# Transposing q and k of the later head pairs as float32r words by way of a DRAM copy, with a rearranged start

## The chip, the cores and the metric

One core of a Trainium2 chip runs the whole program. The metric is the device time of one execution in microseconds (us). The median of three runs of the kernel before is 1066.27 us (1065.2 to 1066.96).

## The reference, cut to what matters

Attention over 4 batches, 8 heads, 576 tokens and head size 64, with a memory term mixed in by a gate, then two feed-forward stages on the 2304 rows that result. All of it is float32.

```python
scores = scale * (q @ k.T)                 # causal, then softmax -> a
local  = a @ v
q_p    = phi(q)                            # elu(q) + 1
mem    = (q_p @ M_prev) / (q_p @ z_prev)
x      = g * mem + (1 - g) * local         # g = sigmoid(beta), per head
h      = relu(x @ w_in);  y = (s * h * h + b) @ w_out
out    = (sigmoid(y @ w_gate) * (y @ w_val)) @ w_out2
```

## The kernel before, in words

The work on attention is cut into 16 jobs, one for each batch and pair of heads. Two heads of 64 make one tile of 128 columns, and the 576 tokens make five blocks (four of 128 and a last of 64, in which the two heads share the partitions). Jobs 0 to 3 (batch 0) are called DIRECT and have their own code (`prep_direct`, L989, `scores_direct`, `products_direct`); jobs 4 to 15 go through `plan_prep` (L541), `plan_scores` and `plan_products`. For each job, `load_raw` (L389) brings q, k and v from DRAM with 64-float rows. `transposed` (L444) then turns the five blocks of q and the five of k on TensorE, with the float32 identity `ident` as the moving operand and the block as the stationary one (L451), into PSUM. ScalarE writes the rounded high half of the result (`q_hi`, `k_hi`), VectorE the remainder (`q_lo`, `k_lo`), both as float32r, and every later product is three float32r matmuls on high and low halves.

The feed-forward products follow: `h_mm` (L320, matmuls at L326), in 128 chunks of 12 matmuls, which are also the filler that TensorE does between attention steps from about 87 us on; y (L1519); then the gate and value products m (L1787) and the output o (L1884). The rectified h goes through a ring of two tiles `r` (L335), each for two chunks, and is stored to DRAM by SyncE (`h_store`, L338).

The order is not written by hand. Each step is put into a `Plan` with its engine, an estimated duration and an urgency; `order()` (L70) plays it through and, whenever an engine is free, takes the most urgent step that is ready by these estimates. The urgencies come from the numbers in `TUNE` (L24). The resulting order of each engine is fixed in the program: a step whose data comes late holds all that stands behind it on its engine, SyncE's queue of DMA issues included. The slots (`slots`, L468) bound how far loads run ahead: two tiles each for raw q and raw k.

Before the plan starts, `load_consts` (L218) issues three small broadcasts from ScalarE's queue (beta, s, b), and computes the gates; `load_consts2` (L377) spreads them with twelve small VectorE copies. The first q (job 0) is loaded from ScalarE's queue behind these three, all other loads from SyncE's.

Of the kernel before, what the change touches and what calls it, by code (L numbers as in the profile page):

```python
# [13 lines left out]
ALU = mybir.AluOpType  # L14
# [142 lines left out]
def attention_moe_kernel(  # L157
# [36 lines left out]
    def dram(name, shape):  # L194
        return nc.dram_tensor(name, shape, F32, kind="Internal").ap()

    r_d = dram("relu_scratch", [DFF, NT])
# [8 lines left out]
    ident = const.tile([P, P], F32, name="ident")  # L206
    nc.gpsimd.memset(ident, 0.0)
    nc.gpsimd.affine_select(
        out=ident, in_=ident, compare_op=ALU.not_equal, fill=1.0, base=0,
        pattern=[[-1, P]], channel_multiplier=1,  # L210
    )
    gt = const.tile([P, H], F32, name="gt")
# [5 lines left out]
    def load_consts():  # L218

        nc.scalar.dma_start(gt, beta.partition_broadcast(P))  # L220
        nc.scalar.dma_start(sb_s, s_in.partition_broadcast(P))
        nc.scalar.dma_start(sb_b, b_in.partition_broadcast(P))
        nc.scalar.activation(gt, gt, AF.Exp, scale=-1.0)
        nc.vector.tensor_scalar(out=gt, in0=gt, scalar1=1.0, scalar2=None, op0=ALU.add)
# [120 lines left out]
    rawqs = [at.tile([P, NQ, P], F32, name=f"rawq{i}", bufs=1) for i in range(2)]  # L345
    rawks = [at.tile([P, NQ, P], F32, name=f"rawk{i}", bufs=1) for i in range(2)]
    rawv = at.tile([P, NQ, P], F32, name="rawv", bufs=1)

    def zero_raw():


        for t in rawks:
            nc.gpsimd.memset(t[LAST:, NQ - 1], 0.0)
        for t in rawqs:
            for e in range(2):
                nc.gpsimd.memset(t[e * LAST : (e + 1) * LAST, NQ - 1, (1 - e) * D : (2 - e) * D], 0.0)
        nc.gpsimd.memset(rawv[: P - LAST, NQ - 1], 0.0)

# [18 lines left out]
    def load_consts2():  # L377
        for e in range(2):
            c = slice(e * NQ, e * NQ + NT4)
            nc.vector.tensor_copy(iom[:, :, c], iomg[:, e::2].unsqueeze(2).broadcast_to([P, NP, NT4]))  # L380
            r = slice(e * LAST, (e + 1) * LAST)
            nc.vector.tensor_copy(iom[r, :, NT4], iomg[r, e::2])
            for dst, src in ((iomu, iomg), (gtu, gt)):
                nc.vector.tensor_copy(
                    dst[:, :, e : 2 * NT4 : 2], src[:, e::2].unsqueeze(2).broadcast_to([P, NP, NT4])
                )
                nc.vector.tensor_copy(dst[r, :, NC - 1], src[r, e::2])

    def load_raw(j, src, dst, ta):  # L389
        b, p, t0, t1 = jobs[j]  # L390
        eng = nc.scalar if src is q and j == 0 else nc.sync
        te = min(t1, NQ - 1)
        d4 = dst if len(dst.shape) == 4 else dst.rearrange("p t (h d) -> p t h d", h=2)
        for e in range(2):
            eng.dma_start(
                d4[:, ta:te, e],
                src[b, 2 * p + e, ta * P : te * P].rearrange("(t p) d -> p t d", p=P),
            )
        if t1 == NQ and src is q:
# [84 lines left out]
    def flip(n):  # L484
        return 112 * n + 30
# [1541 lines left out]
```

## Time and profile before

| | |
|---|---|
| median of 3 runs | 1066.27 us |
| the profiled execution's own time | 1065.1 us |
| its span | 1063.0 us |
| TensorE busy | 1037.5 us, 98% |
| TensorE idle in the span | 25.5 us |
| VectorE, ScalarE, GpSimd busy | 696.1, 564.4, 315.0 us |

The span runs from the first to the last instruction that the profiler recorded. The profiled execution took 2.1 us more than its span and 1.2 us less than the median. Busy times of TensorE are unions of pipelined matmuls, so a group's busy time has a tail of the last matmul in it; the chain of waits tells better how long a group holds the engine.

### The profile page before, as it was taken

What the parts mean: (1) busy time and instruction counts of PE and PEld (TensorE: products, weight loads), DVE (VectorE), ACT (ScalarE), POOL (GpSimd) and SP (SyncE); (2) the same over time, 40 slices, a digit from 0 to 9 for tenths busy, and PEclk for the clock granted to TensorE, in tenths of its full rate; (3) what the DMA queues carried; (4) which work ended last, traced back from release to release, by engine and by line L of the source; (5) the groups of instructions that cost most, each with busy time, mean ns of one, the idle gap of its engine ahead of it and who ended that gap; (6) DMA issues with size and microseconds to landing.
All of it is one profiled execution on the core that took longest, in us unless ns stands there. A gap on an engine that the chain in (4) does not pass through costs nothing.

```text
span 1063.0 us, 18848 instructions
## 1 busy us (share of the span) xinstructions
PE 1037.5 (98%) x6696; PEld 979.9 (92%) x6696; DVE 696.1 (65%) x1424; ACT 564.4 (53%) x1221; POOL 315.0 (30%) x361
## 2 busy tenths in 40 slices
PE   4998999999999999999999999999999999999998
PEld 3887999999999999999999999998899998899986
DVE  4887888866667638669888775778525576155531
ACT  3877778876777748557777673335212243112230
POOL 2244665554343503310400002446102342033200
PEclk9999999999999999999999999999999999999999
DMA  6533444333321129659689977992368830677400
GB/s 154 135 103 91 122 138 123 82 105 87 89 80 57 51 93 320 210 195 331 235 289 364 389 260 261 329 343 79 114 216 256 251 111 30 199 253 256 154 24 36
DMA packets 159693, 186.45 MB, mean 175 GB/s; under 512 B 70256, under 2 KB 135280, under 8 KB 159600
## 3 DMA queue, kind: packets, MB, share of 16 engines
q1 hardware_dynamic: 157952, 184.95, 53.9%
q8 instruction: 53, 0.87, 0.3%
q10 hardware_dynamic: 1648, 0.30, 0.2%
q14 instruction: 40, 0.33, 0.1%
HBM read 138.03 MB, written 47.19 MB: 174 GB/s over the span
## 4 chain that ended last, share of the span: by engine, by line
PE 95%; ACT 2%; DVE 2%; issue 1%; DMA 1%; POOL 0%; ACTq 0%; DVEq 0%; POOLq 0%
PE m L1787 24%; PE h L326 19%; PE y L1519 18%; PE o L1884 14%; PE sc L704 3%; PE o L1251 2%; PE acc L888 2%; PE acc L889 2%; PE pt_B L835 1%; PE sc L730 1%; PE sc L1118 1%; PE kt L451 1%; PE qt L451 1%; PE acc L892 1%; PE pt_D L835 1%
## 5 line engine op out<-in xcount | busy, mean ns | idle before, releaser
L1787 PE MATMUL m<-yt,ws 128*128 128x384 f32 x1512 | 262.8, 334 | 0.0
L1787 PEld LDWEIGHTS m<-yt,ws 128*128 128x128 f32 x1512 | 262.2, 188 | 0.3
L326 PE MATMUL h<-x,w_in 128*128 128x256 f32 (+1 forms) x1536 | 224.9, 300 | 0.0
L326 PEld LDWEIGHTS h<-x,w_in 128*128 128x128 f32 x1536 | 209.2, 190 | 2.9 <-issue 1.8
L1799 DVE TENSOR_TENSOR set<-m,set 128x384 f32<-128x384 f32 x252 | 135.6, 555 | 99.7 <-PE m L1787 91.7
L1884 PE MATMUL o<-w_out,ps 128*128 128x512 f32 x648 | 152.1, 396 | 0.6 <-DVE ps L1874 0.6
L1519 PE MATMUL y<-gh,w_out 128*128 128x384 f32 (+1 forms) x768 | 150.7, 338 | 0.7 <-ACT r L336 0.5
L1884 PEld LDWEIGHTS o<-w_out,ps 128*128 128x128 f32 x648 | 121.7, 188 | 29.9 <-DVE ps L1874 1.0
L1519 PEld LDWEIGHTS y<-gh,w_out 128*128 128x128 f32 x768 | 135.4, 188 | 1.4 <-ACT r L336 0.8
L1809 POOL TENSOR_TENSOR p<-set,set 128x384 f32<-128x384 f32 x72 | 75.6, 1056 | 187.8 <-DVE set L1799 186.8
L278 POOL TENSOR_TENSOR w_out<-raw_w_out,w_out 128x512 fp32r<-128x512 f32 x28 | 37.8, 1350 | 214.3 <-DVE set L1799 127.8
L336 ACT ACTIVATE r<-h 128x320 f32<-128x320 f32 (+1 forms) x128 | 52.3, 410 | 71.5 <-PE h L326 59.1
L684 DVE CUSTOM_DVE_ANT_0 P<-sc,mask 128x256 f32<-128x256 f32 (+4 forms) x144 | 68.4, 514 | 24.1 <-PE sc L704 19.7
L1519 PE MATMUL y<-gl,w_out 128*128 128x384 f32 x384 | 82.9, 337 | 0.0
L1795 ACT COPY set<-m 128x384 f32<-128x384 f32 x36 | 17.3, 481 | 111.5 <-PE m L1787 111.5
L762 POOL TENSOR_SCALAR P<-P,rs 128x384 f32<-128x384 f32 (+4 forms) x108 | 64.7, 621 | 30.4 <-DVE rs L758 18.8
L1504 DVE TENSOR_TENSOR gl<-rr,gh 128x384 fp32r<-128x384 f32 x96 | 57.7, 609 | 22.5 <-PE y L1519 12.5
L1874 DVE TENSOR_TENSOR ps<-p,ps 128x512 fp32r<-128x512 f32 x54 | 46.1, 883 | 35.8 <-ACT ps L1861 35.5
L1519 PEld LDWEIGHTS y<-gl,w_out 128*128 128x128 f32 x384 | 68.6, 188 | 0.0
L746 ACT ACTIVATE P<-P,nm 128x384 f32<-128x384 f32 (+4 forms) x108 | 62.6, 581 | 10.1 <-DVE nm L684 9.8
L1803 ACT ACTIVATE set<-set 128x384 f32<-128x384 f32 x72 | 37.6, 524 | 57.1 <-DVE set L1799 57.1
L1861 ACT CAST ps<-p 128x512 fp32r<-128x512 f32 x54 | 31.9, 620 | 65.8 <-PE o L1884 51.8
(185 smaller groups left out, 1507.2 us busy)
## 6 DMA issues: line engine op xcount, KB each, us to landing
ws<-weight_scratch SPq DMA_DIRECT2D x108, 512.0 KB, 4.6
rr<-relu_scratch SPq DMA_DIRECT2D x96, 192.0 KB, 5.4
weight_scratch<-wp SPq DMA_DIRECT2D x36, 512.0 KB, 6.5
raw_w_out<-in_moe_w_out_dram SPq DMA_DIRECT2D x28, 512.0 KB, 5.6
relu_scratch<-r SPq DMA_DIRECT2D x32, 320.0 KB, 2.7
ws<-weight_scratch SPq DMA_DIRECT2D x36, 256.0 KB, 3.0
raw_w_in<-in_moe_w_in_dram SPq DMA_DIRECT2D x16, 512.0 KB, 4.2
relu_scratch<-r SPq DMA_DIRECT2D x32, 256.0 KB, 2.4
```

The costliest lines, as they stand in the source:

```text
L326: nc.tensor.matmul(t[:, :n], wt[:, wi, c], x[:, xi, c], start=(m == 0), stop=(m == 3 * NK - 1))
L336: nc.scalar.activation(rts[b, c0, f - f % 2][:, f % 2, :n], t[:, :n], AF.Relu)
L684: nc.vector.tensor_tensor_reduce(out=pr, in0=ps, in1=mk, scale=1.0, scalar=3e38, op0=ALU.add, op1=ALU.min, accum_out=nm,)
L746: nc.scalar.activation(pr, pr, AF.Exp, bias=T.pop(("nm", j, e, t)), scale=-1.0, accum_out=T["sums", j][:, col : col + 1],)
L762: nc.gpsimd.tensor_scalar(out=pr, in0=pr, scalar1=T["rs", j, part][:, n : n + 1], scalar2=1.0, op0=ALU.mult, op1=ALU.mult,)
L1504: nc.vector.tensor_tensor(out=gl, in0=r_sb.pop(step)[:, :n], in1=gs[step][0][:, :n].bitcast(F32), op=ALU.subtract,)
L1519: nc.tensor.matmul(accs[wi][d][:, : y.shape[1]], w_out_sb[f][:, x, d], y, start=(f == 0 and x == 0 and y is gh), stop=(f == NF - 1 and y i ...
L1787: nc.tensor.matmul(acc, wt[:, a, k : k + P], yt[:, y, c], start=(m == 0), stop=(m == 3 * K2 - 1),)
L1799: nc.vector.tensor_tensor(out=t[:, o], in0=Z["m", z, x], in1=t[:, i], op=ALU.add)
L1809: engine[TIMES[o]].tensor_tensor(out=p[:, f + HF * OF[o][0], OF[o][1]], in0=Z["set", z][:, o], in1=Z["set", zg][:, o], op=ALU.mult,)
L1874: nc.vector.tensor_tensor(out=part(t, 1, i), in0=src(i), in1=part(t, 0, i).bitcast(F32), op=ALU.subtract,)
L1884: nc.tensor.matmul(Z["zo", z], Z["ps", z, i][:, a, k * P : (k + 1) * P], w_out2_sb[f][:, x].rearrange("p c f -> p (c f)"), start=(i == k = ...
```

## The change

1. **Later jobs (4 to 15).** q and k of a job are first copied from DRAM to DRAM (`copy`, one DMA of 294,912 bytes for each of q and k), then loaded from that scratch into tiles of type float32r. `transposed` sees the type and transposes with a float32r identity (`identr`) into a float32r view of PSUM. phi reads the same words as float32.
2. **One comparison.** For job 4 the first four blocks of k are also transposed in float32 (`again`), and VectorE compares 32 columns of both (`compare`, four small instructions); where they differ, 1e30 is added to b.
3. **DIRECT jobs (0 to 3).** q and k are loaded with four tokens to a partition, in runs of 256 floats instead of 64; the transposes write every fourth column of PSUM (`mixed`), which puts the tokens in order again. In job 0 the transposed q is taken in two parts (four blocks and one). The high half of q comes ahead of the rectified copy on ScalarE.
4. **Constants.** The three broadcasts go to SyncE's queue and into the plan; the twelve copies go to GpSimd (`spread`). `mem_norm`, `norm`, `phi_s` and `rsums` now wait for the gates.
5. **The plan.** all 39 numbers in `TUNE` have new values and three are added, so the order on all engines is played out anew. The estimates of the q and k transposes of the later jobs go from 112 to 58 ns per block.

```diff
@@ transposed
-            nc.tensor.transpose(t[:, c : c + P], src[:, i], ident)
+            o = t[:, i : NT4 * P : NT4] if mixed and i < NT4 else t[:, c : c + P]
+            if src.dtype == F32R:
+                nc.tensor.transpose(o.bitcast(F32R), src[:, i], identr)
+            else:
+                nc.tensor.transpose(o, src[:, i], ident)
@@ load_raw
+        tokens = "(p t) d -> p t d" if j in DIRECT and src is not v else "(t p) d -> p t d"
...
+        if from_q or from_k:
+            dst = raw_of("q" if from_q else "k", j)
+            if j not in DIRECT:
+                dst, src = dst.bitcast(F32), qs_d if from_q else ks_d
...
+    def copy(j, src):
+        b, p = jobs[j][:2]
+        h = slice(2 * p, 2 * p + 2)
+        nc.sync.dma_start((qs_d if src is q else ks_d)[b, h], src[b, h])
@@ plan_load
+            bounce = not direct and src is not v
+            if bounce:
+                add(
+                    "SP", 450, lambda src=src: copy(j, src), u + du + AT["cp"],
+                    reads=[("ld", j - 2)], writes=[(key + "d", j)], late=1900, size=3e5,
+                )
@@ plan_prep
-        add("PE", flip(nt), qt, u + AT["q"], reads=[("rawq", j)],
+        add("PE", 58 * nt + 30, qt, u + AT["q"], reads=[("rawq", j)],
...
+        def again():
+            T["ka", j] = transposed(raw_of("k", j).bitcast(F32), 0, NT4, f"ka{j}")
...
+        if j == NP:
+            add("PE", flip(NT4), again, u + AT["k"], reads=[("rawk", j)], new=[("s", ("ka", j))], late=250)
@@ load_consts
-        nc.scalar.dma_start(gt, beta.partition_broadcast(P))
-        nc.scalar.dma_start(sb_s, s_in.partition_broadcast(P))
-        nc.scalar.dma_start(sb_b, b_in.partition_broadcast(P))
+        nc.sync.dma_start(gt, beta.partition_broadcast(P))
+        nc.sync.dma_start(sb_s, s_in.partition_broadcast(P))
+        nc.sync.dma_start(sb_b, b_in.partition_broadcast(P))
@@ prep_direct
+        parts = [(t0, NT4), (NT4, t1)] if j == 0 else [(t0, t1)]
...
+        add("ACT", act(n) + more, q_hi, u + AT["q"], reads=qts, writes=[("QT", j)])
+        add("ACT", act(n) + more, relu, u + AT["q"], reads=qts, writes=[("phi", j)])
@@ the plan
+    add("SP", 1500, load_consts, AT["lc"], writes=[("gates", 0)], late=1900)
+    add("ACT", 210, gate_exp, AT["gc"], writes=[("gates", 0)])
+    add("DVE", 1000, gates, AT["gc"], writes=[("gates", 0)])
+    for x in range(4):
+        add("POOL", 600, lambda x=x: spread(x), AT["gc"], writes=[("gates", 0)])
...
-    load_consts()
-    load_consts2()
@@ TUNE (some of the 42 values)
-    "mem": -121814.8, ... "ft": -153978.3, "m": 1612.8, ... "relu": -411.9, "wo": 957.8, ... "gv": 152484.7,
+    "mem": -261434.9, ... "ft": -264268.8, "m": -86465.6, ... "relu": -158690.1, "wo": -4845.2, ... "gv": 193.7,
```

## Rows read from the trace of the kernel before

**Rows 1.** The page: busy time by engine, and TensorE in 40 slices

```profile
PE 1037.5 (98%) x6696; PEld 979.9 (92%) x6696; DVE 696.1 (65%) x1424; ACT 564.4 (53%) x1221; POOL 315.0 (30%) x361
...
PE   4998999999999999999999999999999999999998
...
GB/s 154 135 103 91 122 138 123 82 105 87 89 80 57 51 93 320 210 195 331 235 289 364 389 260 261 329 343 79 114 216 256 251 111 30 199 253 256 154 24 36
```

**Rows 2.** Busy time by stage (stretch, length, engines, clock, DMA share, GB/s)

```profile
0.00:9.20 9.20, 0.00 (x0) 0.03 (x1) 2.32 (x17) 1.49 (x2) 4.16 (x22) 1.00 0.51 101
9.20:26.00 16.80, 11.28 (x65) 8.55 (x65) 9.07 (x26) 7.49 (x13) 1.31 (x1) 1.00 0.70 179
26.00:106.00 80.00, 74.75 (x683) 65.90 (x684) 66.26 (x185) 61.21 (x130) 30.55 (x38) 0.98 0.44 111
106.00:372.00 266.00, 265.42 (x2120) 250.40 (x2119) 194.51 (x486) 198.43 (x501) 133.14 (x168) 1.00 0.33 93
```

**Rows 3.** What TensorE waited for, whole span (us, times, longest)

```profile
PE qt L451 <- DMA mem<-in_z_prev_dram: 9.2, 1, 9.2
PE ret L1063 <- DVE phi L1019: 3.0, 1, 3.0
PE pt_B L835 <- POOL P L762: 2.1, 1, 2.1
PE kt L451 <- DVE KT L1040: 1.5, 1, 1.5
```

**Rows 4.** q and k transposes: the tile views, and the chain around 321 us

```profile
L451 PE MATMUL qt<-ident,rawq x80: 270/273/477, 9.2 to 321.6; 128*128 128x128 f32 x80
...
L451 PE MATMUL kt<-ident,rawk x80: 270/273/476, 15.8 to 329.9; 128*128 128x128 f32 x80
...
321.35 0.55 PE qt L451 x5
...
329.62 0.55 PE kt L451 x5
```

**Rows 5.** Timeline of TensorE at 308 us: float32r matmuls with 128 columns

```profile
308.35 0.22 PE L888 MATMUL acc<-PT_A,VHL 128*128 128x128 f32 x1
308.41 0.22 PE L889 MATMUL acc<-PT_A,VHL 128*64 128x128 f32 x1
308.47 0.33 PE L892 MATMUL acc<-FS,mst 128*128 128x256 f32 x1
```

**Rows 6.** Timeline of the first 20 us, the queues and the first steps

```profile
0.74 0.45 ACTq L220 DMA_DIRECT2D gt<-in_beta_dram  x1
...
1.23 0.52 ACTq L221 DMA_DIRECT2D sb_s<-in_moe_s_dram  x1
...
1.78 0.52 ACTq L222 DMA_DIRECT2D sb_b<-in_moe_b_dram  x1
...
2.33 0.46 ACTq L395 DMA_DIRECT2D rawq<-in_q_dram  x1
...
4.06 0.61 SPq L406 DMA_DIRECT2D rawk<-in_k_dram  x1
...
5.72 0.38 ACTq L395 DMA_DIRECT2D rawq<-in_q_dram  x1
...
5.98 0.35 SPq L433 DMA_DIRECT2D mem<-in_M_prev_dram  x1
...
6.49 1.17 ACTq L401 DMA_DIRECT2D rawq<-in_q_dram  x2
...
9.21 1.30 PE L451 MATMUL qt<-ident,rawq 128*128 128x128 f32 x5 [9.21 <-DMA mem<-in_z_prev_dram]
...
19.91 2.61 PE L1118 MATMUL sc<-KT,QT 64*128 64x128 f32 x18
```

**Rows 7.** DMA view of the first 12 us (KB, us to landing), rawq tile view

```profile
rawq<-in_q_dram ACTq DMA_DIRECT2D x2, 128.0 KB, 4.4
...
rawq<-in_q_dram ACTq DMA_DIRECT2D x2, 16.0 KB, 2.6
...
sb_b<-in_moe_b_dram ACTq DMA_DIRECT2D x1, 0.5 KB, 4.7
...
DMA to landing us min/median/max: 2.0/2.4/5.3
```

**Rows 8.** TensorE around 98 us: busy and clock (columns as Rows 2), and timeline

```profile
92.00:96.00 4.00, 2.35 (x21) 1.80 (x19) 2.06 (x7) 2.86 (x11) 0.41 (x1) 1.00 0.20 68
96.00:100.00 4.00, 2.36 (x15) 2.15 (x16) 3.12 (x7) 3.47 (x7) 4.00 (x9) 0.87 0.00 0
100.00:104.00 4.00, 4.00 (x24) 3.83 (x24) 3.15 (x6) 3.65 (x7) 1.66 (x2) 0.71 0.35 77
...
97.62 1.31 PE L835 MATMUL pt_B<-ident,P 128*128 128x128 f32 x10 [2.09 <-POOL P L762]
```

**Rows 9.** Stores of h between 106 and 372 us (tile view), and large scratch stores (DMA view)

```profile
L340 SPq DMA_DIRECT2D relu_scratch<-r x43: 359/367/546, 108.2 to 369.6; - x43
...
weight_scratch<-wp SPq DMA_DIRECT2D x36, 512.0 KB, 6.5
```

More of the change, by code (lines that the diff above doesn't have):

```diff
@@ L204, in attention_moe_kernel @@
     w1 = w1s.enter_context(tc.tile_pool(name="w1", bufs=16, side="left"))
-    ident = const.tile([P, P], F32, name="ident")
-    nc.gpsimd.memset(ident, 0.0)
+    identr = const.tile([P, P], F32R, name="identr")
+    ident = identr.bitcast(F32)
+    eye = stage.tile([P, NK * P], F32, tag="f", name="eye", bufs=FB)[:, :P]
+    nc.gpsimd.memset(eye, 0.0)
     nc.gpsimd.affine_select(
-        out=ident, in_=ident, compare_op=ALU.not_equal, fill=1.0, base=0,
+        out=eye, in_=eye, compare_op=ALU.not_equal, fill=1.0, base=0,
         pattern=[[-1, P]], channel_multiplier=1,
     )
+    nc.vector.tensor_copy(identr, eye)
     gt = const.tile([P, H], F32, name="gt")
@@ L343, in h_store, with raw_of, make_raw @@
         )
-    rawqs = [at.tile([P, NQ, P], F32, name=f"rawq{i}", bufs=1) for i in range(2)]
-    rawks = [at.tile([P, NQ, P], F32, name=f"rawk{i}", bufs=1) for i in range(2)]
     rawv = at.tile([P, NQ, P], F32, name="rawv", bufs=1)
-    def zero_raw():
[L352 to L356, printed above, removed]
+    raws = {}
+    def raw_of(c, j):
+        return raws[c, j % 2, j in DIRECT]
+    def make_raw(j):
+        for c in "qk":
+            t = raws[c, j % 2, j in DIRECT] = at.tile(
+                [P, NQ, P], F32 if j in DIRECT else F32R, tag=f"raw{c}{j % 2}", name=f"raw{c}{j}",
+                bufs=1,
+            )
+            t = t if j in DIRECT else t.bitcast(F32)
+            if c == "k":
+                nc.gpsimd.memset(t[LAST:, NQ - 1], 0.0)
+                continue
+            for e in range(2):
+                r = slice(e * LAST, (e + 1) * LAST)
+                nc.gpsimd.memset(t[r, NQ - 1, (1 - e) * D : (2 - e) * D], 0.0)
+    def zero_raw():
+        make_raw(0)
+        make_raw(1)
         nc.gpsimd.memset(rawv[: P - LAST, NQ - 1], 0.0)
@@ L404, in load_raw @@
         elif t1 == NQ:
-            lo = 0 if src is k else P - LAST
+            lo = 0 if from_k else P - LAST
             eng.dma_start(
@@ L530, in plan_load @@
                 lambda src=src, dst=dst, ta=ta: load_raw(j, src, dst, ta), u + du,
-                new=[(key, (key, j))], late=1900, size=(t1 - ta) * P * 800,
+                reads=[(key + "d", j)] if bounce else [],
+                writes=([(key, j)] if first and src is not v else []) + ([("ld", j)] if src is k else []),
+                new=[] if first and src is not v else [(key, (key, j))], late=1900, size=(t1 - ta) * P * (500 if direct else 800),
             )
@@ L578, in k_lo @@
             )
[L580 removed]
+        add("PE", 58 * t1 + 30, kt, u + AT["k"], reads=[("rawk", j)],
             new=[(bank(t1), ("kt", j)), ("KT", ("KT", j))], late=250)
+        if j == NP:
+            add("PE", flip(NT4), again, u + AT["k"], reads=[("rawk", j)], new=[("s", ("ka", j))], late=250)
+            add("DVE", 900, compare, u + AT["k"], reads=[("ka", j), ("kt", j), ("gates", 0)], writes=[("same", j)])
         add("ACT", act(nk), k_hi, u + AT["k"], reads=[("kt", j)], writes=[("KT", j)])
@@ L646, in plan_prep @@
         )
-        add("DVE", 1200, phi_s, w, reads=[("phit", j)], new=[("nrm", ("nrm", j))])
+        add("DVE", 1200, phi_s, w, reads=[("phit", j), ("gates", 0)], new=[("nrm", ("nrm", j))])
         add("POOL", **port(1260), fn=phi_n, urgency=w, reads=[("nrm", j)], writes=[("phi", j)])
@@ L805, in plan_scores @@
                 "DVE", 450, lambda part=part, cols=cols: rsums(part, cols), w + part,
-                reads=sums[part] + [("sums", j)], new=[(f"rs{part}", ("rs", j, part))],
+                reads=sums[part] + [("sums", j), ("gates", 0)], new=[(f"rs{part}", ("rs", j, part))],
             )
@@ L992, in prep_direct, with relu @@
         u = 100 * j
+        parts = [(t0, NT4), (NT4, t1)] if j == 0 else [(t0, t1)]
         def qt():
-            T["qt", j] = transposed(rawqs[j % 2], t0, t1, f"qt{j}")
+            T["qt", j] = [
+                (slice(a * P, c * P), transposed(raw_of("q", j), a, c, f"qt{j}_{a}", True)) for a, c in parts
+            ]
         def q_hi():
+            d = T["QT", j] = at.tile([P, 2, NQ * P], F32R, tag="QT", name=f"QT{j}")
+            for c, x in T["qt", j]:
+                nc.scalar.activation(d[:, 0, c], x, AF.Copy, scale=-SCALE)
+        def relu():
             f = at.tile([P, NQ, 2, D], F32, tag="phi", name=f"phi{j}", bufs=1)
             f = T["phi", j] = f.rearrange("p t h d -> p (t h d)")
-            c = slice(t0 * P, t1 * P)
-            nc.scalar.activation(f[:, c], T["qt", j], AF.Relu, scale=-1.0)
-            d = T["QT", j] = at.tile([P, 2, NQ * P], F32R, tag="QT", name=f"QT{j}")
-            nc.scalar.activation(d[:, 0, c], T["qt", j], AF.Copy, scale=-SCALE)
+            for c, x in T["qt", j]:
+                nc.scalar.activation(f[:, c], x, AF.Relu, scale=-1.0)
         def phi_a():
@@ L1100, in prep_direct @@
         add(
-            "DVE", 1450, mem_norm, w, reads=[("ret", j, 0), ("ret", j, 1)], writes=[("MX", j)],
+            "DVE", 1450, mem_norm, w, reads=[("ret", j, 0), ("ret", j, 1), ("gates", 0)], writes=[("MX", j)],
         )
```

95 lines of the change are left out of this document (61 added, 34 removed), and 15 rows, old and new, of the table TUNE.

## The prediction

> **What bounds the kernel now.** I first read the page's busy times: TensorE is busy 1037.5 of 1063.0 us, no other engine over 65%, and its 40 slices are full but for the first, the fourth and the last [rows 1]. So a change pays in two ways only: it takes work off TensorE, or it fills some of its 25.5 us of idle time. The stage table shows where those lie: 9.2 us before the first matmul, 5.5 up to 26 us, 5.3 up to 106 us, and only 0.6 in the 266 us of the later jobs [rows 2]; the remaining 4.9 lie behind, which the change hardly touches. The list of waits names the large ones: 9.2 us for the first q, 3.0 for phi of job 0, 2.1 for GpSimd's normalized P, 1.5 for the k of job 0 [rows 3]. (The first wait is put down to a z_prev load; the load that the transposes read is q's, whose last issue ends at 7.66 [rows 6].)
>
> **The transposes.** They are counted 80 for q and 80 for k, five of each for 16 jobs; 12 jobs change, so 120 blocks. In the chain of waits a group of five float32 transposes holds TensorE 0.55 us, 110 ns a block [rows 4]. The kernel before has no float32r transpose. The nearest row is a float32r matmul with 128 moving columns and its own weights: starts at 308.35, 308.41 and 308.47, so 60 ns [rows 5]. I take 60, as the operand type, the 128 columns and the weight load for each matmul are those of the new transpose. Saved: 120 x 50 ns = 6.0 us. Bounds: 0, if the mode keeps the float32 price, and 120 x 110 = 13.2, if it cost nothing. As TensorE is busy 265.4 of 266 us while most of them run [rows 2], and fills every gap with h chunks, what is saved there is saved whole.
>
> The Trainium skill, page "TensorE: Matmul & The Clock Gate", section "Back-to-back issue gap", gives a stream of weight load and matmul at 128 columns about 81 ns each; by that the saving would be 29 ns x 120 = 3.5 us, an estimate from that page. The 60 ns of this trace are below it, and the trace decides.
>
> The comparison adds four float32 transposes, 4 x 110 = 0.44 us, and four small VectorE instructions, which hide (VectorE is busy 66.3 of 80 us there [rows 2]); without that cover they would delay one k_lo by under a microsecond. The 32 transposes of the DIRECT jobs that write every fourth column: 0, as the count and operand stay; a price for the strided write is not in the trace, bounds 0 and the price of a transpose again, 32 x 110 = 3.5 us.
>
> **The first load.** ScalarE's queue issues three broadcasts from 0.74 to 2.30 us, then the first half of q at 2.33, the second half only at 5.72, behind the exponential of the gates, which needs beta landed, and the two tails until 7.66 [rows 6]. The change takes the broadcasts and the exponential away: four issues of 0.46, 0.38 and 1.17 us from 0.74 on end at 2.75. A tail of 16 KB lands 2.6 us after issue [rows 7], so q is there at about 5.2 against 9.2: minus 4.0 us. Bounds: if a half of 128 KB takes the longest 5.3 us of the tile's loads, the second, issued at 1.2, lands at 6.5, minus 2.7; if each takes the shortest 2.0 [rows 7], the last tail, issued at 2.2, lands at 4.2, minus 5.0. The longer runs of the load (a quarter of the packets) are counted as nothing beyond that.
>
> **Behind it.** From the first transpose at 9.21 to the first scores at 19.91 lie 10.7 us [rows 6], with both idle waits of 3.0 and 1.5 us in them [rows 3], since the memory product of job 0 was placed ahead of k. In the change q's high half no longer stands behind the rectified copy, 0.7 us on ScalarE, but two parts cost one more fixed share each time. How the new order places the memory product I can't read from the trace. I take a third of the 4.5 us, minus 1.5; bounds 0 and minus 4.5.
>
> **The gap at 92 to 100 us.** TensorE idles 1.65 + 1.64 = 3.3 us there, the granted clock then falls to 0.87 and 0.71 of full speed over two 4 us stretches [rows 8]: part of them ran at 1.2 instead of 2.4 GHz, and the missing shares, 0.13 and 0.29 of 4 us, are 0.52 + 1.16 = 1.7 us of work lost. Together 5.0 us. The new urgencies (relu far ahead, so the two h banks come free sooner) may fill it or open another like it. I take minus 1; bounds plus 3, minus 5.
>
> **What is moved and added elsewhere.** The three broadcasts on SyncE's queue stand ahead of weights, M_prev and q of job 1; each takes about 0.5 us to issue, 1.5 in all, and that queue stands still from 4.67 to 5.98, between the first two k and M_prev [rows 6]: 1.3 of the 1.5 us fit there, and the rest delays M_prev of job 0 by 0.2. The gates are ready later: a broadcast takes 4.7 us to land [rows 7]. The waiting instruction is `mem_norm` on VectorE, behind which k_lo and the softmax of the first jobs stand; I count 0, since 5.5 us of TensorE's time up to 26 us are idle anyhow, bound plus 1.5. The twelve spread copies leave VectorE, where they ended before it had anything else to do: 0. The 24 DRAM copies are 24 more issues on SyncE, about 0.4 us each like h's stores [rows 9], and their bytes meet a DMA share of 0.33 in the stage of the later jobs [rows 2]: 0, as the loads run one to two jobs ahead. Each load now waits on SyncE for its copy, and behind it stand the stores of h; the rival below prices that.
>
> **The sum.** -6.0 + 0.44 - 4.0 - 1.5 - 1.0 = -12.1 us. From the profiled execution's own 1065.1 that gives 1053.0; the median of the runs is 1.2 above that execution, so I predict **1054.2 us**.
>
> **The rivals.**
> *Float32r transposes cost what float32 ones do.* Then the change doesn't do what it says: 6.0 us come back, 1060.2. For it: no row shows the mode. Against: every float32r matmul here with this shape is at 60 ns.
> *The early start is given back.* The first scores still wait for something that does not come sooner (M_prev, w_in, GpSimd), so that 4.0 and 1.5 shrink to 2.7 or less and a gap like the one at 98 us grows by up to 3: -6.0 + 0.4 - 2.7 + 0 to 3, thus 1058 to 1061, at worst (no gain at the start) 1064.
> *The copies hold SyncE's queue: slower.* A DMA from DRAM to DRAM is not in the trace. The busiest slice moves 389 GB/s over 16 engines [rows 1]. If a copy whose outermost size is 2 (heads) ran on two of them, at 389 / 8 = 48.6 GB/s, the 294,912 bytes take 6.1 us, and the 2.6 of a small load to land [rows 7] make 8.7. The 43 stores of h lie 6.2 us apart [rows 9], and the ring of two tiles covers one such distance: from a hold of 6.2 us on, ScalarE's relu waits for a store, then TensorE for a bank. 8.7 - 6.2 = 2.5 us for each of 24 copies is 60 us at worst, 30 if half of them find a store behind them: 1084. Against it: the copied heads lie side by side, so it need not be cut by heads, the plan issues the load only when it believes the copy landed, and a 512 KB scratch store lands in 6.5 us [rows 9]. The Trainium skill, page "DMA: Bandwidth & Descriptors", section "Why a DMA increments its semaphore by 16 and not by 1", says that a DMA is spread over the largest number of engines up to 16 that divides the slowest dimension of both sides, which would make it two here. No row of the trace before shows such a transfer, so it stays a rival.
>
> **How the numbers follow.** Less than 0.2%, 2.1 us, can't be told from no change. The forecast gets 0.63, same-price transposes 0.12, the start given back 0.13 (0.06 of it within 0.2%), held copies 0.12. The forecast's own spread is 1048 to 1059 (transposes 6.0 to 7, start 2.7 to 5.0, waits 0 to 4.5, gap -5 to +3, not all at once). The range 1047 to 1064 takes in the first two rivals but for the worst end; some 2 in 10 lie outside. Faster 0.82, same 0.06, slower 0.12.
>
> **What would show it.** Right: groups of five transposes of the later jobs at about 0.30 us in the chain, first transpose near 5 us, first scores several us before 19.9, no TensorE wait of over 1 us between 106 and 372 us, h's stores still some 6 us apart. Wrong: those groups still at 0.55; TensorE waiting on relu or for raw q or k in the later jobs; a new gap with a lowered clock before 106 us.

## The result, and the profile after

The changed kernel takes 1076.38 us (median of 9 runs, 1070.9 to 1079.85) against 1066.96 (9 runs, 1064.9 to 1069.74) for the kernel before on the same chip: ratio 1.0087, 95% interval 1.0066 to 1.0109. It is slower by 9.4 us, and 1054.2 had been predicted, with 1064 as the upper end. The profiled execution is the fastest of the nine, 1070.9 us with a span of 1069.1 (1065.1 and 1063.0 before), so its trace shows 6.1 us of the loss of 9.4.

The page of the changed kernel: busy times, TensorE in 40 slices, and the granted clock in the same slices.

```profile
PE 1041.1 (97%) x6700; PEld 982.2 (92%) x6700; DVE 695.2 (65%) x1419; ACT 566.4 (53%) x1223; POOL 313.5 (29%) x379
...
PE   4888999999999999999999999999999999999998
...
PEclk9899999999999999999999999999999999999999
```

TensorE is busy 3.6 us longer than before [rows 1], although 120 of its transposes are cheaper. Slices 2 and 3 are less full, and slice 2 has a lower clock. The busy times by stage (columns as in [rows 2]) say the same in numbers:

```profile
0.00:9.20 9.20, 0.00 (x0) 0.00 (x0) 1.66 (x7) 1.49 (x2) 5.96 (x34) 1.00 0.47 122
9.20:26.00 16.80, 11.49 (x68) 9.13 (x68) 11.04 (x29) 9.00 (x18) 1.30 (x1) 1.00 0.70 168
26.00:106.00 80.00, 72.22 (x633) 62.42 (x633) 62.94 (x175) 55.96 (x115) 29.22 (x38) 0.93 0.60 156
106.00:372.00 266.00, 265.16 (x2124) 250.86 (x2122) 189.61 (x475) 197.07 (x490) 127.17 (x167) 0.99 0.37 106
```

Against [rows 2] the stage of 26 to 106 us holds 2.5 us less of TensorE work, 50 matmuls fewer, and its clock is 0.93 where it was 0.98. The missing share of the clock is 0.07 x 80 = 5.6 us of work, against 1.6 before. Over the whole span the mean clock is 0.992 against 0.998: (0.008 - 0.002) x 1069 = 6.4 us, about the 6.1 by which the span grew. The rest of the account nearly cancels: TensorE's idle time is 28.0 us (span less busy) against 25.5, and its busy time without the clock's share is 1032.5 us against 1035.4, which is about what the cheaper transposes save. The other eight runs have mean clocks of 0.982 to 0.989 and times of 1074.08 to 1079.85, so the time goes with the clock, about 1 us for each 0.001.

Waits of TensorE, in the list of waits (as [rows 3]):

```profile
PE qt L488 <- DVE identr L217: 9.8, 1, 9.8
PE ret L1144 <- DMA mem<-in_z_prev_dram: 2.8, 1, 2.8
PE pt_A L1292 <- ACT P L1239: 1.7, 1, 1.7
PE kt L486 <- DVE QT L608: 1.7, 1, 1.7
PE sc L1199 <- DVE nm L752: 1.5, 2, 1.1
PE o L1332 <- issue: 1.4, 1, 1.4
```

The waits for phi, for GpSimd's P and for the k of job 0 [rows 3] are gone, and six of 0.8 to 1.7 us stand between 23 and 108 us. The kernel before had three over 0.8 us there: the 2.1 of [rows 3] and

```profile
PE pt_A L1211 <- ACT P L1158: 1.2, 1, 1.2
PE ft L451 <- DVE QT L556: 1.2, 1, 1.2
```

What follows such a wait is seen in stretches of 2 us around the wait of o at 37.7 (columns as above):

```profile
36.00:38.00 2.00, 0.57 (x6) 0.31 (x3) 2.00 (x7) 2.00 (x6) 0.00 (x0) 1.00 0.68 155
38.00:40.00 2.00, 2.00 (x20) 2.00 (x19) 1.22 (x5) 0.64 (x2) 0.00 (x0) 0.94 0.76 172
40.00:42.00 2.00, 2.00 (x12) 2.00 (x11) 0.84 (x2) 1.47 (x3) 0.73 (x1) 0.50 0.71 162
42.00:44.00 2.00, 2.00 (x16) 2.00 (x15) 0.00 (x0) 0.80 (x3) 0.00 (x0) 0.70 0.74 191
```

TensorE is busy for 0.57 us of two; some 2 us after it starts again the granted clock is 0.50, the 1.2 GHz level, for about 3.4 us, and TensorE is full all the while. Four such stretches stand in this profile, at 26 to 30, 40 to 44, 74 to 78 and 105 to 112 us; before there was one, at 99 to 103 [rows 8].

The transposes: tile views of q and k (min, median, max in ns), and groups of five in the chain of waits, where a group of before holds TensorE 0.55 us [rows 4]. L486 is the float32r form.

```profile
L486 PE MATMUL qt<-identr,rawq x60: 222/248/278, 78.4 to 330.4; 128*128 128x128 f32 x60
...
L486 PE MATMUL kt<-identr,rawk x60: 222/248/308, 82.7 to 337.9; 128*128 128x128 f32 x60
...
89.30 0.39 PE qt L486 x5
...
330.25 0.44 PE qt L486 x5
...
337.82 0.37 PE kt L486 x5
```

So a block costs 74 to 88 ns in the chain, and one transpose lasts 248 ns where it lasted 273 [rows 4]: 25 ns less, half of what I took.

The start, in the timeline (as [rows 6]):

```profile
2.18 0.64 SPq L250 DMA_DIRECT2D raw_w_in<-in_moe_w_in_dram  x1
...
5.62 1.34 SPq L423 DMA_DIRECT2D rawk<-in_k_dram  x2
...
8.43 0.43 DVE L270 TENSOR_SCALAR raw_w_in<-raw_w_in 128x512 int32<-128x512 int32 x1 [2.40 <-DMA raw_w_in<-in_moe_w_in_dram]
...
9.51 0.22 DVE L217 CAST identr<-eye 128x128 fp32r<-128x128 f32 x1
...
9.78 1.33 PE L488 MATMUL qt<-identr,rawq 128*128 128x128 f32 x5 [9.78 <-DVE identr L217]
...
10.32 0.50 SPq L466 DMA_DIRECT2D mem<-in_M_prev_dram  x1
...
14.94 1.98 PE L1144 MATMUL ret<-mem,phi 64*128 64x65 f32 x16 [2.77 <-DMA mem<-in_z_prev_dram]
...
18.52 1.97 PE L1199 MATMUL sc<-KT,QT 64*128 64x128 f32 x14
```

The first transposes wait for the identity, 9.78 us, when q has landed (its four loads at 5.6, 6.7, 6.9 and 8.7 us): its one cast stands on VectorE behind a step on w_in, which waits 2.40 us for a weight load that SyncE issued ahead of k. Then ret waits for the memory tile (M_prev and z_prev), which SyncE issues from 10.32 us on, behind k and w_in. The first scores come at 18.52 instead of 19.91.

### The profile page after: what moved, and what is told of

It reads as the page before. It is cut to its first block, busy times and chain, and to the rows that moved or that the text cites. A ratio compares the mean times of both kernels' runs of the same rounds, so it can differ in the third digit from the quotient of the medians.

```text
span 1069.1 us, 18900 instructions
## 1 busy us (share of the span) xinstructions
PE 1041.1 (97%) x6700; PEld 982.2 (92%) x6700; DVE 695.2 (65%) x1419; ACT 566.4 (53%) x1223; POOL 313.5 (29%) x379
## 4 chain that ended last, share of the span: by engine, by line
PE 95%; DVE 2%; ACT 1%; DMA 1%; issue 1%; SPq 0%; DVEq 0%
PE m L1868 24%; PE h L336 20%; PE y L1600 18%; PE o L1965 14%; PE sc L772 3%; PE acc L956 2%; PE o L1332 2%; PE acc L957 2%; PE pt_B L903 1%; PE sc L798 1%; PE acc L960 1%; PE sc L1199 1%; PE pt_D L903 1%; PE pt_A L903 1%; PE ft L488 1%
## 5 line engine op out<-in xcount | busy, mean ns | idle before, releaser
L830 POOL TENSOR_SCALAR P<-P,rs 128x384 f32<-128x384 f32 (+4 forms) x108 | 62.0, 597 | 41.6 <-DVE rs L826 41.6
L1585 DVE TENSOR_TENSOR gl<-rr,gh 128x384 fp32r<-128x384 f32 x96 | 58.0, 613 | 21.8 <-PE y L1600 14.9
L814 ACT ACTIVATE P<-P,nm 128x128 f32<-128x128 f32 (+4 forms) x108 | 62.5, 580 | 10.2 <-DVE nm L752 9.9
```

Of the source, the lines that this page charges most:

```text
L814: nc.scalar.activation(pr, pr, AF.Exp, bias=T.pop(("nm", j, e, t)), scale=-1.0, accum_out=T["sums", j][:, col : col + 1],)
L830: nc.gpsimd.tensor_scalar(out=pr, in0=pr, scalar1=T["rs", j, part][:, n : n + 1], scalar2=1.0, op0=ALU.mult, op1=ALU.mult,)
L1585: nc.vector.tensor_tensor(out=gl, in0=r_sb.pop(step)[:, :n], in1=gs[step][0][:, :n].bitcast(F32), op=ALU.subtract,)
```

## The experiments

Thirteen kernels ran. They ran in four sets, each with the kernel before on the same chip, to which the ratios are; its medians there were 1066.12, 1065.19, 1065.39 and 1064.98 us.

**The late identity.** The changed kernel with the cast on GpSimd:

```diff
-    nc.vector.tensor_copy(identr, eye)
+    nc.gpsimd.tensor_copy(identr, eye)
```

> The changed kernel with one edit: GpSimd, not VectorE, converts the identity, right behind its making, so that no weight step stands ahead of it; every other order is as it was. Theory A (the new order of steps leaves TensorE idle between 26 and 112 us, its clock falls, and that is the loss): the first transpose comes at about 5.6 us instead of 9.8, but the memory product of job 0 still waits for M_prev until about 14.9, so the time falls by 0 to 2 us, to 1074 to 1076, with the gaps and lowered clock still there. Rival C (the late identity gave the early start back and shifted everything off its plan): the time falls by 4 us or more, to 1072 or less, and the clock is above 0.99.

Measured: 1078.89 us, ratio 1.0122 (1.0102 to 1.0142), clocks 0.982 to 0.986. Neither number held. The first transposes came at 6.80 us, not 5.6, and then waited for the last of q; the first scores came at 17.93. The time is 2.5 us above the changed kernel: at waits of 0.9 and 1.1 us, the same two as there at 71 and 73 us, a stretch at the 1.2 GHz level lasts 20 us, where the changed kernel's lasts 3.4.

```profile
6.80 1.08 PE L488 MATMUL qt<-identr,rawq 128*128 128x128 f32 x4 [6.80 <-DMA rawq<-in_q_dram]
8.85 0.45 PE L488 MATMUL qt<-identr,rawq 128*128 128x128 f32 x1 [0.96 <-DMA rawq<-in_q_dram]
...
74.00:94.00 20.00, 19.23 (x102) 17.48 (x103) 11.64 (x29) 8.86 (x17) 5.99 (x7) 0.50 0.39 90
```

The late identity is seen in the trace but is not the loss.

**The transposes alone.** The order and the copies of the change, all transposes in float32:

```diff
-                nc.tensor.transpose(o.bitcast(F32R), src[:, i], identr)
+                nc.tensor.transpose(o, src[:, i].bitcast(F32), ident)
```

> The changed kernel with the same order and the same copies, but the later jobs' q and k transposed in float32. In the changed kernel a group of five holds TensorE 0.37 to 0.44 us in the chain of waits against 0.55 in float32. Theory A, in which TensorE is the bound there: 24 groups by 0.15 us are 3.6 us more, 1080 us. Rival B (the copies and the loads behind them set the pace in the later jobs): no change, 1076.

Measured: 1077.38 us, ratio 1.0111 (1.0091 to 1.0132), clocks 0.986 to 0.991, between the two numbers. Only 1 us above the changed kernel by the medians; but the clock differs from run to run, and at 0.989 two runs took 1077.95 and 1078.25 us where two of the changed kernel took 1074.08 and 1074.17. The price of the transposes needed a comparison at one clock, which came later.

**The order alone.** The order of the change on all engines, with the data path of before: no copies, 64-float runs, plain transposes.

```diff
-        tokens = "(p t) d -> p t d" if j in DIRECT and src is not v else "(t p) d -> p t d"
+        tokens = "(t p) d -> p t d"
...
-            if j not in DIRECT:
-                dst, src = dst.bitcast(F32), qs_d if from_q else ks_d
...
-        nc.sync.dma_start((qs_d if src is q else ks_d)[b, h], src[b, h])
+        return
...
-            o = t[:, i : NT4 * P : NT4] if mixed and i < NT4 else t[:, c : c + P]
+            o = t[:, c : c + P]
```

> The changed kernel's order on all five engines, but q and k loaded as before: no DRAM copies, runs of 64 floats, tiles and transposes in float32. Constants, late identity and the comparison (which here compares float32 with float32) stay. Theory A: the order alone makes the loss, so the time stays at or above the changed kernel's, 1076 to 1081 (3.6 us for float32 transposes on top), with TensorE's clock lowered in several stretches between 26 and 112 us. Rival B (the copies and rearranged loads are at fault): back to 1067 or at most 1069.

Measured: 1073.44 us (1073.27 to 1073.99), ratio 1.0075 (1.0059 to 1.009), clock 0.990 in each of five runs. Its stage of 26 to 106 us:

```profile
26.00:106.00 80.00, 74.10 (x624) 63.88 (x622) 61.04 (x172) 54.50 (x113) 27.92 (x36) 0.89 0.43 109
```

The order of the steps, with the moved constants, the late identity and the comparison but no copies and no rearranged loads, costs 7.3 us, and the lowered clock comes with it. Rival B fell; theory A's number, 1076 or more, did not hold either. In the profile it is nearly all clock: TensorE idles 26.1 us (25.5 before), while the mean clock of 0.990 misses 10.7 us of 1072.1 (2.1 before). The kernel of the second experiment has the same order and float32 transposes, and adds the copies, the longer runs and the strided writes: it is 3.9 us slower (1.0111 against 1.0075, each good to 0.002). In the two profiles 3.3 us of that is there at the k transposes of job 4 (86.9 against 83.6 us), so ahead of most copies. Which of the three costs it was not tried.

**The new operations in the old order.** The kernel before with copies (issued one job ahead, behind the loads of the job), float32r tiles and transposes, and the identity cast on GpSimd; the order on TensorE, VectorE and ScalarE is that of before.

```diff
+        if (from_q or from_k) and NP <= j + 1 < NJ:
+            b, p = jobs[j + 1][:2]
+            h = slice(2 * p, 2 * p + 2)
+            nc.sync.dma_start((qs_d if from_q else ks_d)[b, h], source[b, h])
...
+            if src.dtype == F32R:
+                nc.tensor.transpose(t[:, c : c + P].bitcast(F32R), src[:, i], identr)
```

> The kernel before with its order on TensorE, VectorE, ScalarE unchanged, and added to it the copies (each issued one job ahead, right behind the load of the same operand of the job before) and the float32r transposes of the later jobs; GpSimd makes the identity. No comparison, no rearranged start. Theory A: 3.6 us less than before, 1063, the gaps as before. Rival B: the waits for copies appear in this order too, 1068 or more. Price of 60 ns a block, as I predicted: 1061.

Measured: 1066.27 us (1063.1 to 1071.92), ratio 1.0002 (0.9986 to 1.0019), between the two theories' numbers. No loss without the new order, and no gain that shows among clocks of 0.990 to 0.998. (The copies are issued at other places here than in the change, so this clears copies as such, not those of the change.)

**Work in the waits.** If the lowered clock follows from TensorE standing still, then matmuls that do nothing useful, put into its queue ahead of the waiting groups, must keep the clock up. A fill goes ahead of the group with that number in TensorE's order, into a PSUM bank of h that is free then; nobody reads it. First on the changed kernel, at seven places:

```diff
+        fills = {8: 7, 21: 6, 64: 4, 65: 5, 103: 7, 104: 2, 105: 4}
...
+                if count in fills:
+                    t = ps_h.tile([P, 512], F32, tag="h", name=f"fill{count}")
+                    for i in range(fills[count]):
+                        nc.tensor.matmul(t[:, :P], ident, ident, start=True, stop=True)
```

> The changed kernel as it is, with 35 extra 128-column float32 matmuls of the identity with itself into a bank that nobody reads, put into TensorE's queue ahead of seven groups that wait between 25 and 108 us (7 ahead of pt_A at 25.2, 6 ahead of o at 37.7, 4 and 5 ahead of the scores at 71.6 and 73.8, 7, 2 and 4 ahead of kt, xt and ft at 104, 105 and 107). They add no useful work and take no wait away. Theory A (the new order loses time because TensorE's waits are followed by stretches at the 1.2 GHz level): with something to do in those waits the granted clock of 26 to 112 us goes from 0.90 back to 0.97 or more, the mean clock of a run from 0.982 to 0.992 to 0.994 or more, and the time from 1076 to 1066 to 1070 us. Rival K (the lower clock comes from the kind or the amount of work in the new order, not from its waits): no gain, or a loss by the added work; 1076 to 1080 us with a mean clock of 0.983 to 0.990.

Measured: 1075.75 us (1075.18 to 1076.38), ratio 1.0095 (1.0077 to 1.0112), clock 0.991 or 0.992 in every run. By the time, theory A fell, and rival K's numbers are just missed. The stages of its profile say something else (columns as in [rows 2]):

```profile
26.00:47.00 21.00, 19.58 (x189) 17.63 (x187) 14.71 (x43) 14.47 (x28) 3.46 (x7) 1.00 0.72 180
47.00:51.00 4.00, 2.09 (x16) 1.41 (x15) 2.80 (x6) 2.04 (x5) 2.28 (x3) 1.00 0.75 207
51.00:68.00 17.00, 17.00 (x106) 15.60 (x103) 8.79 (x26) 6.97 (x14) 3.42 (x9) 0.50 0.37 96
68.00:106.00 38.00, 36.83 (x329) 31.25 (x330) 31.46 (x85) 28.22 (x59) 15.99 (x15) 1.00 0.58 155
```

All four old stretches are gone, and one of 17 us stands behind three waits that were not filled, of 0.4, 0.6 and 0.9 us between 47 and 51. At half the clock it costs 8.5 us of work, as much as the four had cost together (three of 3.4 us and one of 6.8). Two other waits without a fill, 1.0 us at 42 and 1.2 at 118, have no stretch behind them. I then filled all of these, with 55 matmuls in all (the expectation below miscounts them as 53):

```diff
-        fills = {8: 7, 21: 6, 64: 4, 65: 5, 103: 7, 104: 2, 105: 4}
+        fills = {8: 7, 21: 6, 33: 4, 39: 2, 40: 3, 41: 4, 64: 4, 65: 5, 67: 2, 103: 7, 104: 2, 105: 4, 112: 5}
```

> The changed kernel with 53 extra identity matmuls: the 35 of e5_fill, and 18 more ahead of the waits that e5_fill left or showed (4 ahead of ka at 42.9, 2, 3 and 4 ahead of pt_B, pt_D and pt_C at 47.9, 49.0 and 50.7, 2 ahead of pt_B at 81.2, 5 ahead of acc at 118.9). In the profile of e5_fill the four stretches at the 1.2 GHz level that stood behind the filled waits (26, 40, 74 and 105 us) were gone, and one of 16.5 us stood behind the waits of 47.5 to 51. Theory A': such a stretch follows a TensorE wait, its length is not set by that wait, and the loss of the new order is made of them: with no wait over 0.4 us left after 16 us, no stretch is left, the mean clock is 0.998 or more, and the time 1076 less 8 to 9, that is 1066 to 1069 us. Rival K (another cause lowers the clock in the first 120 us, and the stretch moves wherever waits are left or not): a stretch of 10 us or more appears though no wait stands ahead of it; clock 0.990 to 0.993, 1074 to 1077 us.

Measured: 1068.17 us (1067.45 to 1068.96, 12 runs), ratio 1.0019 (1.0009 to 1.0029), clock 1.0 in eleven runs and 0.999 in one. Theory A' held in time and clock; one wait of 0.5 us was left (pt_C at 51 us), and no stretch stands behind it. Its busy time, the fills' share of it, and two stages of its profile:

```profile
PE 1047.6 (98%) x6810; PEld 989.1 (93%) x6810; DVE 695.1 (65%) x1419; ACT 565.4 (53%) x1223; POOL 313.8 (29%) x379
...
L2081 PE MATMUL fill<-identr 128*128 128x128 f32 x110 | 14.9, 280 | 0.0
...
26.00:106.00 80.00, 78.00 (x723) 68.33 (x721) 63.81 (x178) 55.73 (x116) 30.92 (x40) 1.00 0.60 159
106.00:372.00 266.00, 265.94 (x2142) 251.62 (x2141) 190.31 (x477) 198.30 (x494) 125.42 (x165) 1.00 0.37 105
```

55 matmuls without use made the changed kernel 7 to 8 us faster. The kernel runs at full clock, and is still slower than before. It did not get back all that the clock had cost: in the median run of the changed kernel the clock misses 0.014 x 1074.6 = 15 us. But idle time and fills together are 19.4 + 14.9 = 34.3 us here, 6.3 more than the 28.0 of idle time in the changed kernel's profile, and 15 - 6.3 = 8.7 is about the 8.2 measured. Some of the 6.3 us are the fills themselves, where one outlasts its wait: ka starts behind its fill at 43.06 us, while its last k load has landed at 42.68. By the releases that the trace shows this makes some 2 us over all fills, an estimate. The rest would be waits that the slower TensorE did not meet; that is argued and not tried.

**The same in the old order.** The kernel before, and the float32r kernel in the old order, with fills in their own waits:

```diff
+        fills = {8: 4, 17: 3, 103: 4, 104: 8}
```

> The kernel before, float32 transposes and no copies, with the same 19 extra identity matmuls at the same places as e10_old_fill_f32r. Theory A': no stretch at the lower level, 1063 to 1064.5 us with clock 0.999 or more, 1 to 2 us under the kernel before. The difference to e10_old_fill_f32r is the price of the transposes in the old order: 2.6 to 4.3 us by the groups of five in the traces; about 0 if the time of the transposes is taken back by the waits beside them. Rival K: 1065 to 1066 us, no difference to the kernel before.

> The old order with float32r transposes and copies and 19 extra identity matmuls in its waits: 4 ahead of pt_A at 25.8, 3 ahead of o at 32.5, 4 ahead of ft at 94.6, 8 ahead of pt_B at 97.5. Theory A': no stretch at the lower level; the time is that of the best runs of e6_old_fill, 1061.5 to 1063 us, with clock 0.999 or more, 2 to 4 us under the kernel before and under e11_before_fill by what the float32r transposes are worth at full clock (24 groups by 0.11 to 0.18 us: 2.6 to 4.3 us, less what other waits take back). Rival K: 1064 to 1066 us with clock 0.996 to 0.998, as without the extra work.

Measured: before with fills 1063.64 us (1063.05 to 1064.16), ratio 0.998 (0.997 to 0.999), clock 0.999 or 1.0 in all 12 runs; with float32r 1063.03 us (1061.83 to 1069.59), ratio 0.9976 (0.9961 to 0.9991), clock 1.0 or 0.999 in 8 of 11. So the kernel before lost about 2 us to its one stretch, as theory A' had it. The difference between the two, 0.6 us, is under the 2.6 to 4.3 expected of the transposes. Both kernels beat the kernel before and the changed one. An earlier form with the fills at 94 and 97 us alone:

> The old order with float32r transposes and copies (the kernel of the run e4_old_order_f32r, 1066.27 us) plus 12 extra matmuls of the identity in the one place where that order has TensorE wait after 26 us: 4 ahead of ft at 94.6 and 8 ahead of pt_B at 97.5. Theory A: the stretch at 98 to 101.3 us, granted 0.50 to 0.65 there, runs at full clock, which gives back half of its 3.3 us; about 1.5 us less, 1064 to 1065.5 us. Rival K: nothing, 1066 us; if the extra work itself delays the transposes behind it, 1067 us.

Measured: 1064.62 us, ratio 0.9988 (0.9976 to 0.9999), as theory A had it. In its profile the stretch at 98 us is gone, but ret stood 2.0 us at 47 to 49 and another of 3.4 us followed.

```profile
46.73 0.66 ACT L262 ACTIVATE f_w_in<-raw_w_in 128x512 f32<-128x512 f32 x1 [3.60 <-DMA raw_w_in<-in_moe_w_in_dram]
...
49.02 1.10 PE L1094 MATMUL ret<-mem,phi 64*128 64x65 f32 x14 [2.04 <-ACT PT_B L1259]
```

ret waits for a copy of ScalarE, which stands behind a weight step that waited 3.6 us for its load; in e4_old_order_f32r the same step waited 1.4 us and ran at 44.35. So a load that lands late in one execution is enough for a stretch.

**The price of the transposes at full clock.** The filled kernel in the new order with float32 transposes (the edit of the second experiment):

> The kernel of e9_fill_all (1068.17 us, clock 1.0: the new order with all its larger waits filled) with its 120 float32r transposes in float32 again; copies and order stay. Theory T (at full clock the float32r transposes are worth what the trace gives each, 273 less 247 ns by 120, 3.1 us, less what waits beside them take back): 1070 to 1071.5 us. Rival (the time of the transposes is taken back by the waits of this order, as most of it seems to be in the old order, where e10_old_fill_f32r and e11_before_fill differ by 0.6 us): 1068 to 1069 us.

Measured: 1071.37 us (1071.15 to 1071.89), ratio 1.0053 (1.0039 to 1.0066), clock 0.999 or 1.0. Theory T held: 3.2 us by the medians, 3.6 by the ratios, against 120 x 26 ns = 3.1 from the tile views. In the old order the same comparison gives 0.6 us by the medians. Between the k transposes of job 4 and of job 15 the float32r kernel is 2.1 us shorter there too (68.7 to 327.0 against 67.8 to 328.2), but it reaches job 4's 0.9 us later, while the first copies share the transfers of the start.

**The first q load.** The kernel before with the constants issued behind the first q tile (`first_q` is filled by its `load_raw`):

```diff
-    load_consts()
-    load_consts2()
     with tc.manual_schedule():
         for n in plan.order():
             plan.tasks[n][2]()
+            if first_q:
+                first_q.clear()
+                load_consts()
+                load_consts2()
```

> The kernel before with one edit at its start: the three constant loads, the exponential of the gates and their VectorE steps are issued behind the first q tile's four loads instead of ahead of them; the order is the old one otherwise, and the transposes are float32. Theory S (the prediction's own term of 4.0 us: the first q load holds the start): the q loads issue from 0.7 instead of 2.3 and 5.7 us, the first transposes run at 5.2 to 6.2 us instead of 9.2, the first scores at 16 to 17 instead of 19.9, and the time is 2.5 to 4 us less, 1062 to 1063.5 us. Rival G (given back before 26 us): ret then waits for M_prev or for VectorE's phi, the first scores move by less than 1.5 us, and the time is 1065 to 1066.5 us.

Measured: 1064.56 us, ratio 0.9987 (0.9978 to 0.9997), between the two numbers; its timeline:

```profile
5.45 1.30 PE L454 MATMUL qt<-ident,rawq 128*128 128x128 f32 x5 [5.45 <-POOL vals L429]
...
11.14 0.81 DVE L1022 SCALAR_TENSOR_TENSOR phi<-qt,phi 128x640 f32<-128x640 f32 x1
...
12.01 1.33 PE L1066 MATMUL ret<-mem,phi 64*128 64x65 f32 x10 [5.26 <-DVE phi L1022]
```

The first transposes come 3.8 us sooner than in [rows 6], but VectorE now does the steps of the gates ahead of phi, and ret waits 5.3 us for phi instead of 3.0 [rows 3]. 1.5 us are left at ret, which began at 13.49 before, and still at the k of job 4 (66.4 against 67.9); at the end of the run it is 0.6, since the stretch behind the gap at 95 us is longer there (6.8 us, 3.4 before).

With fills and float32r as well, once with much work in the start and once with little:

```diff
+        fills = {0: 14, 1: 10, 3: 5, 8: 4, 103: 4, 104: 8}
```

> The kernel of e6_old_fill with the edit of e7_first_q, and extra matmuls of the identity in the waits of the start too: 14 ahead of the first transposes, 10 ahead of ret, 5 ahead of the second kt, 4 ahead of the first pt_A. Theory A and S together: the sum of both gains and some 2 us more, since the groups of five transposes at the start (1.30 to 1.33 us each) and ret (2.45 us) then run at the full clock; 1058 to 1061 us. If S falls but A holds, 1062 to 1064; if both fall, 1066 to 1068 us.

Measured: 1066.44 us, ratio 1.0011 (1.0 to 1.0023), clocks 0.990 to 0.995, the number for both theories fallen. TensorE came sooner to o, and waited there for the first v load:

```profile
28.00:31.00 3.00, 0.02 (x1) 0.00 (x0) 1.73 (x3) 1.89 (x5) 0.00 (x0) 0.94 0.84 222
31.00:47.00 16.00, 15.81 (x78) 14.73 (x79) 5.88 (x19) 5.15 (x11) 2.20 (x3) 0.50 0.58 147
```

The wait of 3.2 us was followed by 17 us at 0.50, and one of 1.3 us for phi at 10.6 by 3.4 us. The mild form:

```diff
+        fills = {8: 3, 17: 5, 103: 4, 104: 8}
```

> The kernel of e10_old_fill_f32r (1063.03 us) with the edit of e7_first_q: constants behind the first q tile's loads. Extra identity matmuls: 3 ahead of the first pt_A, 5 ahead of o, which waits for the first v load, 4 ahead of ft and 8 ahead of pt_B; none ahead of the first transposes. In e7_first_q the first transposes came 3.7 us earlier, VectorE's phi only 1.5, because the exponential of the gates and fourteen VectorE steps now stood ahead of QT and phi, and the gaps of 93 to 96 us came 1.4 us earlier; then a longer stretch at the 1.2 GHz level took that back. Theory S' (the start is worth 1.5 us, not 4.0, once the clock is held): 1061 to 1062 us, clock 1.0, which would be the fastest of all kernels here. Rival G (the early start ends in the wait for the first v load near 30 us): 1062.5 to 1063.5 us.

Measured: 1063.45 us, ratio 0.9989 (0.9974 to 1.0004), against 1063.03 and 0.9976 without the early start. Theory S' fell; G's number held, though the wait came at ret at 45.8 us (0.7 us, then a stretch of 3.4), not at o. The early start is worth nothing at the end of the run.

## Why the prediction was wrong, point by point

**The step that failed** is the term for the changed order: minus 1 (plus 3 to minus 5) for the gap at 92 to 100 us, and 0 for what is moved and added elsewhere. I counted the order as one gap that might be filled or opened again. The runs show it as the largest term, with the clock that goes with it. At full clock and with float32 transposes the new order, with its copies and its start, is 1.0053 against 0.998 for the old one, both with fills: 0.0073 x 1066 = 7.8 us. Float32r takes back 1.0053 - 1.0019, 3.6 us. The clock, in what fills give back of it, adds the rest: 1.0087 - 1.0019 = 7.2 us in the changed kernel, less the 2.1 that the kernel before loses to it itself. 7.8 - 3.6 + 7.2 - 2.1 = 9.3 us is the measured loss, but it must be: the terms are differences of the same ratios, each good to one or two microseconds, so the sum divides the loss and does not test it.

The 7.8 us are not the order's waits alone. The new order has 55 fills in it and the old one 19, which outlast their waits by some 2 and 1 us (the same estimate); and the copies and rearranged loads, 3.9 us between the second and the third experiment, are in it too. That the order by itself loses is shown by the third experiment, 7.3 us without any of these, there nearly all by the clock.

What the order does is read from the traces: with fills taken off, TensorE has useful work for 100.9 us of the first 130 in e9_fill_all and for 109.0 in e10_old_fill_f32r (fills take 14.9 and 5.1 us there). One place shows how (VectorE and TensorE of the changed kernel around 105 us):

```profile
104.39 0.94 DVE L270 TENSOR_SCALAR raw_w_in<-raw_w_in 128x512 int32<-128x512 int32 x1
105.37 0.95 DVE L273 SCALAR_TENSOR_TENSOR raw_w_in<-raw_w_in 128x512 int32<-128x512 int32 x1
106.25 0.74 DVE L641 TENSOR_TENSOR KT<-kt,KT 128x576 fp32r<-128x576 f32 x1
...
107.05 1.33 PE L488 MATMUL ft<-identr,phi 128*128 128x128 f32 x5 [0.84 <-DVE KT L641]
```

Two steps on a weight tile, 0.95 us each, stand on VectorE ahead of the step that frees ft's bank. The last step on their tile runs on GpSimd only at 110.95 us; the plan put them there. Which of the 42 numbers does it was not tried.

**The clock** stood in my text only as a price of the old gap (1.7 us) and as one of the signs of being wrong, "a new gap with a lowered clock before 106 us"; that sign came four times. I gave it no term of its own, so that the sum held neither the 7.2 us nor the spread of 9 us between runs of one kernel, which is larger than any single saving I forecast.

**The transposes**, -6.0: the mechanism was right, the size was off. The nearest row, float32r matmuls 60 ns apart [rows 5], was not near enough; a block costs 74 to 88 ns, and the saving was 3.2 to 3.6 us. The rule I set beside it, the Trainium skill, page "TensorE: Matmul & The Clock Gate", section "Back-to-back issue gap", about 81 ns and, as an estimate, 3.5 us, agrees with these runs; the row that I preferred to it does not. The comparison, +0.44, is 0.44 us in the chain, as priced; its VectorE steps hid.

**The first load**, -4.0, and **behind it**, -1.5: the first transposes came 0.6 us later, not 4 sooner, and the first scores 1.4 sooner, which later waits took back. The load itself was mis-sized: its four issues ran from 0.73 to 3.40 us and landed at 5.6 to 8.7, outside my bounds for the last of them (4.2 to 6.5), as e1_ident_pool shows in the transposes at 6.80 and 8.85. The order alone, with the runs of 64 floats, has the last of q at 9.1 us, so the longer runs are not what delays it. I had looked for the next late thing among M_prev, w_in and GpSimd only in a rival; it was the identity behind w_in on VectorE, then M_prev on SyncE, and in the old order phi behind the gates. This rival had the mechanism for the start; its 1058 to 1064 kept a saving elsewhere that was not there.

**The copies**: the rival that was slower had the direction and not the mechanism. What it priced (two engines, 8.7 us for a copy) did not happen: in the trace a copy is carried as 16 pieces of 18,432 bytes, copies of 288 KB land in 3.4 and 3.7 us by the DMA view, and no TensorE wait between 120 and 372 us is put down to a raw load.

```profile
k_scratch<-in_k_dram SPq DMA_DIRECT2D x12, 288.0 KB, 3.4
q_scratch<-in_q_dram SPq DMA_DIRECT2D x12, 288.0 KB, 3.7
```

The rule that I had cited, page "DMA: Bandwidth & Descriptors" of the Trainium skill, section "Why a DMA increments its semaphore by 16 and not by 1", goes by the dimension as the instruction carries it; I had taken that for the 2 heads, and it is 16. Zero was not quite right either: the 0.9 us lost ahead of job 4 in the old order fall in the time of the first copies, and in the new order copies, strided writes and longer runs cost 3.9 us together. What each of them costs or gains was not tried by itself.

## What to carry to other kernels

When a change plays out a whole order anew, the order is a term of its own: measure it alone, with the old operations in it, before the operations are judged, and compare runs at equal clocks. On an engine that sets the end, count a wait twice, once for its length and once for the lowered clock that can follow it; a few matmuls without use in the queue ahead of a waiting group tell the two apart, and here they are also worth having (2.1 us off the kernel before). And a load that comes sooner is worth what the next late thing leaves of it: here 3.8 us at the first transposes, 1.5 at ret, nothing at the end.

## What the runs showed of the hardware

- The length of a stretch at 1.2 GHz does not follow from the wait ahead of it: about 3.4 us behind the 1.4 us of o at 37.7 and behind 2.0 in e6_old_fill, but 17 behind three waits of 0.4 to 0.9 in e5_fill and behind 3.2 in e8_first_q_fill. At the same two waits of 0.9 and 1.1 us, for the scores at 71 to 75 us, it is 3.4 us in the changed kernel, 10 with float32 transposes and 20 in e1_ident_pool. TensorE was busy for nine tenths or more of each.
- The same program has runs with and without a stretch: the kernel before took 1063.5 us at a mean clock of 1.0 and 1068.5 at 0.993. With the waits filled its 12 runs lie within 1.1 us, so the spread is that of the clock.
- A float32r transpose of 128 by 128 holds TensorE 74 to 88 ns in a stream, a float32 one 110 [rows 4], and float32r matmuls of the same size were 60 ns apart [rows 5].
- In the first 20 us of the kernel before the clock column reads 1.00, while a group of five float32 transposes takes 1.30 us there [rows 6] and 0.55 later [rows 4]. In e8_first_q_fill, where fills keep TensorE busy from 2.24 us on, the group at 7.61 us holds it for 0.55 (the next fill starts at 8.16):

```profile
2.24 5.54 PE L2029 MATMUL fill<-identr 128*128 128x128 f32 x28 [2.24 <-POOL identr L216]
7.61 0.71 PE L485 MATMUL qt<-identr,rawq 128*128 128x128 f32 x5
8.16 2.40 PE L2029 MATMUL fill<-identr 128*128 128x128 f32 x20
```

The same group takes its later price there, behind 5.4 us of fills; so the slow groups at the start are TensorE's own, and the clock column does not show them.
